# Attention steps inside five product stages: an order written out by hand for TensorE, VectorE and ScalarE

## The chip, the cores and the metric

One core of a Trainium2 chip. The metric is the device time of one launch in microseconds, the median of several runs. The kernel works on five engines that run beside each other: TensorE (matmuls and transposes), VectorE, ScalarE, GpSimd, and SyncE, which only issues transfers. Each takes its own list of instructions in order, and they wait for each other through semaphores.

## What is computed

Attention with a window and sinks, and then a product of two projections, projected again. In the reference (cut):

```
pos = np.arange(S)
keep = (pos[None, :] < n_sink) | ((rel >= 0) & (rel < window))
scores = np.where(keep, scale * q @ k.T, -1e9)
a = np.exp(scores - max); a = a / (a.sum(-1) + 1e-9)
x = (a @ v).transpose(0, 2, 1, 3).reshape(B * S, H * D)
return (x @ w_a) * (x @ w_b) @ w_out
```

B = 4 batches, H = 8 heads, S = 768 positions of D = 64, 4 sinks, a window of 128; so x is 3072 x 512, the hidden width 1536, all float32. To keep float32 accuracy every operand of a product is split in a high and a low part, and three partial products (high high, high low, low high) are summed.

## The kernel before

The 3072 rows are cut into eight chunks, given in tiles of 128 rows (`CHUNKS`; batch, first tile, number of tiles): (0,0,4), (0,4,2), (1,0,3), (2,0,3), (1,3,3), (2,3,3), (3,0,3), (3,3,3). The kernel runs eight **product stages**, one for each chunk, and in each of them the attention of the chunk that follows; only the attention of the first chunk stands ahead, and the last stage has none beside it. The third to seventh stage have 384 rows each.

A product stage (`moe`) goes over the hidden width in twelve blocks j. For each j there are three **groups** of matmuls: a (12 of 384 columns into PSUM tile a, L769), b (the same into tile b), and o (9 of 512 columns into three tiles that hold the output, L778), which belongs to the block before, j - 1. Between them ScalarE copies a to an SBUF tile g (L788), VectorE multiplies it by b (L794), ScalarE casts it to gh (L797), and GpSimd subtracts to get gl (L799; VectorE for the last two blocks). There is one buffer of g, so the copy of the next a waits until gl is done.

The attention of a chunk is a Python generator; `between(s)`, called behind each group, takes steps of it. A step works on **units** (one head and one query tile of 128, 24 in a chunk) in different phases:

- scores: two matmuls s (L485), an s tile in PSUM; the mask (L491) and the maximum with it (L493) on VectorE; exp on ScalarE (L495); the inverse of the sum on VectorE (L497, L498); the scaling on ScalarE (L503) and the scaling of the eight sink columns to sc (L504).
- transposes, two steps later: T (L524) into PSUM tile t. ScalarE copies it within the tile, rounded (L527), and to p (L530); VectorE makes the high part of the product operand pt (L528), the rest (L531) and the low part (L532). These joined units are those of query tile 2 and above; those of tiles 0 and 1 have one or two T (L539), one ScalarE copy (L542) and one VectorE subtraction (L543).
- av, once for a head: matmuls into tile av (L555), and xf from them by a ScalarE copy (L560) and one or two VectorE additions (L561, L563).
- skt and sk, for four heads together: the sink columns transposed (L570; into the PSUM tile that s uses), split (L573 to L575), and multiplied by the sinks' values (L581, added at L583).

All T of a stage use one PSUM bank, s has one bank, av has one. GpSimd rounds and splits the keys, queries and values of a coming head (`prep_kq`, `prep_v`: qh, ks, ql, ks, vv, vv, and vs for every fourth head; L382, L385).

The third, fourth, ... stage differ in the chunk beside them: attention of tiles 0 to 2 (light: 8 units of each tile) in the third and sixth stage, of tiles 3 to 5 (joined: all units) in the fourth, fifth and seventh. The light ones also have loads and checks of the weights (`check_weight`: a reduction on VectorE, a square on ScalarE).

What sets the order of each engine is a scheduler (Tile's): it takes the program's instructions with their dependencies and its own estimates of their durations, and puts an instruction wherever it expects the engine to be free. So matmuls of attention may stand inside a group of products.

Of the kernel before, what the change touches and what calls it, by code (L numbers as in the profile page):

```python
# [31 lines left out]
BIG = 3.0e38  # L32
# [47 lines left out]
def general_path(tc, ident, val, kT, qT, vB, wa, wb, wo, out):  # L80
# [143 lines left out]
class Fast:  # L224
# [14 lines left out]
    def consts(self):  # L239
        nc, cp = self.nc, self.cp  # L240
        self.m0 = cp.tile([P, P], F32, name="m0")
        self.m1 = cp.tile([P, SW], F32, name="m1")
        self.mg = cp.tile([P, SW], F32, name="mg")
        self.rel = rel = self.at.tile([P, SW], F32, tag="p", name="rel")
        self.col = col = self.at.tile([P, SW], F32, tag="p", name="col")
        it = dict(allow_small_or_imprecise_dtypes=True)
        s, b = slice(P, P + NS), slice(P + NS, SW)
        nc.gpsimd.iota(rel[:, b], pattern=[[-1, P]], base=0, channel_multiplier=1, **it)
        nc.gpsimd.iota(rel[:, :P], pattern=[[-1, P]], base=P, channel_multiplier=1, **it)
        nc.gpsimd.iota(rel[:, s], pattern=[[1, NS]], base=0, channel_multiplier=0, **it)  # L250
# [9 lines left out]
        self.pt, self.kr, self.no_gpsimd, self.banks = None, {}, False, ("t",)  # L260
        self.wt, self.raw, self.wf, self.temp, self.unchecked = {}, {}, {}, None, []

    def masks(self, val):

# [119 lines left out]
    def rest(self, o, i, high):  # L384
        (self.nc.vector if self.no_gpsimd else self.nc.gpsimd).tensor_tensor(o, i, high.bitcast(F32), op=ALU.subtract)  # L385
# [70 lines left out]
    def parts_split(self, b, t0, nt, xf, alone, heads, bank):  # L456
# [127 lines left out]

        return do_prep, scores, transposes, av, sinks_t, sinks_av

    def parts_exact(self, b, t0, nt, xf, alone, heads, bank):

        nc = self.nc
        tag = f"{b}_{t0}"  # L590
        s0 = max(t0 - 1, 0)
        nb = t0 + nt - s0
        kw = nb * KB - NS
        late = [i for i in range(nt) if t0 + i >= 2]
        units = [(h, i) for h in heads for i in range(nt)]
        preps, state, sc, vss, pts, skt = {}, {}, {}, {}, {}, {}
# [155 lines left out]
            xs.append((xh, xl))  # L752
        return xs

    def moe(self, row, nt, xf, between, weights_ahead, last, weights_split):
# [24 lines left out]

        prev = None
        for j in range(NJ):
            if last and j == NJ - 2:
                self.ok = self.verdict(self.ps.tile([1, P], F32, tag="s", name="gp"))
            weights_ahead(3 * j)
            pa = half("a", j)
            g = self.mo.tile([P, max(n, 3 * P)], F32, tag="g", name=f"g{tag}_{j}", bufs=1)
            nc.scalar.copy(g[:, :n], pa[:, :n])  # L788
            between(3 * j)
            if last and j == NJ - 1:  # L790
                self.tc.mark_branch_hint_location("general", hint="LikelyTaken", engines=mybir.ALL_ENGINES)
            weights_ahead(3 * j + 1)
            pb = half("b", j)
            nc.vector.tensor_tensor(g[:, :n], pb[:, :n], g[:, :n], op=ALU.mult)  # L794
            gh = self.mo.tile([P, max(n, 3 * P)], F32R, tag="gh", name=f"gh{tag}_{j}")
            gl = self.mo.tile([P, max(n, 3 * P)], F32R, tag="gl", name=f"gl{tag}_{j}")
            nc.scalar.copy(gh[:, :n], g[:, :n])  # L797
            e = nc.gpsimd if weights_split and j < NJ - 2 else nc.vector
            e.tensor_tensor(gl[:, :n], g[:, :n], gh[:, :n].bitcast(F32), op=ALU.subtract)  # L799
            between(3 * j + 1)  # L800
            weights_ahead(3 * j + 2)
            if prev is not None:
                project(*prev)
# [12 lines left out]
    def run(self, scalars, verdict):  # L816
        chunks = CHUNKS
# [35 lines left out]
        b, t0, nt = chunks[0]  # L853
# [11 lines left out]
        for c, (b, t0, nt) in enumerate(chunks):  # L865
            gen = None
            if c + 1 < len(chunks):
                nb, nt0, nnt = chunks[c + 1]
                nxf = self.new_xf(c + 1)

                self.banks = ("t", "o2") if nt == 2 else ("t",)
                if c == 1:
                    self.join_masks()
                gen = (self.attention if c else self.attention_of_two)(nb, nt0, nnt, nxf)
                steps = H * nnt + 6
            taken = [0]
# [22 lines left out]
            self.moe(b * S + t0 * P, nt, xf, between, ahead, c + 1 == len(chunks), c > 1)  # L899
            if gen is not None:  # L900
                for _ in gen:
                    pass
                xf = nxf
# [74 lines left out]
```

## Time and profile before

| | us |
|---|---|
| median of 3 runs (from 793.3 to 794.84) | 794.43 |
| the profiled execution | 793.14 |
| its span, first to last instruction | 791.4 |

The profiled execution is 1.3 us below the median, and 1.7 us of it lie outside its span. The mean granted clock of TensorE is 0.998 of full speed. A group of matmuls in the profile has a modelled end; a start is measured. The third product stage starts at 243.0 us of the span, the fourth at 334.7, the fifth at 429.7, the sixth at 524.8, the seventh at 615.4, the eighth at 710.6.

### The profile page before, as it was taken

The numbers are of one execution on the slowest core, as the hardware profiler recorded it, in microseconds if no ns is written. First come the engines' busy times: TensorE is split into PE (matmuls) and PEld (weight loads), VectorE is DVE, ScalarE is ACT, GpSimd is POOL, SyncE is SP. The second block draws the span as 40 slices with busy tenths as digits, with TensorE's granted clock in tenths as the row PEclk, the third lists the DMA queues.
The fourth block names the chain that finished last, engine by engine and source line by source line (L and its number), as shares of the span: only waits on it lengthen the run. The fifth ranks groups of instructions, "written<-read, shape, count | busy, mean of one in ns | idle before, by whom it ended". The sixth has DMA issues, their size and how long they took to land.

```text
span 791.4 us, 13783 instructions
## 1 busy us (share of the span) xinstructions
PE 774.1 (98%) x4349; PEld 680.7 (86%) x4349; DVE 516.8 (65%) x1759; ACT 477.8 (60%) x1485; POOL 291.6 (37%) x400
## 2 busy tenths in 40 slices
PE   8999999989999999999999999999999999999997
PEld 5768777779799999998889889999999988989996
DVE  6888889977874675467773777636665478643321
ACT  5867577747765776466663766546764566644431
POOL 1110000146652564355660756416445466201110
PEclk9999999999999999999999999999999999999999
DMA  9877400242121332312111111112333112005511
GB/s 321 291 254 278 180 17 1 75 142 58 48 77 41 101 121 91 119 53 62 45 58 51 45 45 48 48 50 86 122 119 101 54 55 64 28 24 185 176 55 43
DMA packets 44573, 75.84 MB, mean 96 GB/s; under 512 B 4592, under 2 KB 24016, under 8 KB 44496
## 3 DMA queue, kind: packets, MB, share of 16 engines
q1 hardware_dynamic: 41440, 69.40, 27.0%
q10 hardware_dynamic: 3024, 5.51, 1.9%
q8 instruction: 36, 0.59, 0.3%
q14 instruction: 41, 0.34, 0.1%
q0 software_dynamic: 32, 0.00, 0.0%
HBM read 68.60 MB, written 6.29 MB: 95 GB/s over the span
## 4 chain that ended last, share of the span: by engine, by line
PE 84%; DVE 10%; ACT 3%; issue 1%; DMA 0%; POOL 0%; DVEq 0%; ACTq 0%; POOLq 0%
PE b L769 23%; PE a L769 23%; PE o L778 22%; PE s L485 4%; PE av L555 4%; PE t L524 2%; PE s L631 2%; PE av L685 1%; PE t L539 1%; DVE wf L343 1%; DVE wf L336 1%; PE t L668 1%; DVE g L794 1%; DVE gl L799 1%; DVE w L353 1%
## 5 line engine op out<-in xcount | busy, mean ns | idle before, releaser
L769 PE MATMUL a<-xh,w 128*128 128x384 f32 (+2 forms) x768 | 215.8, 342 | 0.8 <-ACT w L348 0.8
L769 PE MATMUL b<-xh,w 128*128 128x384 f32 (+2 forms) x768 | 214.6, 341 | 0.0
L778 PE MATMUL o<-w,gh 128*128 128x512 f32 x576 | 186.7, 402 | 0.7 <-ACT gh L797 0.7
L769 PEld LDWEIGHTS a<-xh,w 128*128 128x128 f32 x768 | 138.6, 188 | 6.2 <-ACT w L348 1.1
L769 PEld LDWEIGHTS b<-xh,w 128*128 128x128 f32 x768 | 138.9, 189 | 3.9 <-issue 0.3
L799 POOL TENSOR_TENSOR gl<-g,gh 128x384 fp32r<-128x384 f32 x60 | 61.0, 1016 | 188.4 <-ACT gh L797 186.1
L769 PE MATMUL b<-xl,w 128*128 128x384 f32 (+2 forms) x384 | 130.1, 339 | 0.0
L769 PE MATMUL a<-xl,w 128*128 128x384 f32 (+2 forms) x384 | 129.4, 337 | 0.0
L794 DVE TENSOR_TENSOR g<-b,g 128x384 f32<-128x384 f32 (+2 forms) x96 | 53.2, 554 | 107.2 <-PE b L769 96.7
L778 PEld LDWEIGHTS o<-w,gh 128*128 128x128 f32 x576 | 104.1, 189 | 19.4 <-ACT gh L797 1.3
L778 PE MATMUL o<-w,gl 128*128 128x512 f32 x288 | 114.9, 400 | 0.6 <-DVE gl L799 0.6
L788 ACT COPY g<-a 128x384 f32<-128x384 f32 (+2 forms) x96 | 45.5, 474 | 71.8 <-PE a L769 66.2
L797 ACT CAST gh<-g 128x384 fp32r<-128x384 f32 (+2 forms) x96 | 49.2, 512 | 64.2 <-DVE g L794 62.1
L769 PEld LDWEIGHTS a<-xl,w 128*128 128x128 f32 x384 | 72.4, 189 | 2.7
L495 ACT ACTIVATE p<-p,st 128x264 f32<-128x264 f32 (+1 forms) x152 | 65.5, 431 | 14.2 <-DVE st L493 12.9
L769 PEld LDWEIGHTS b<-xl,w 128*128 128x128 f32 x384 | 72.5, 189 | 1.6
L382 POOL TENSOR_SCALAR ks<-kr 64x400 fp32r<-64x400 f32 (+1 forms) x48 | 28.9, 603 | 107.7 <-DVE pt L543 105.4
L778 PEld LDWEIGHTS o<-w,gl 128*128 128x128 f32 x288 | 54.3, 188 | 13.7 <-DVE gl L799 1.8
L382 POOL TENSOR_SCALAR qh<-qr 128x384 fp32r<-128x384 f32 x48 | 24.9, 518 | 103.9 <-PE s L485 96.5
L385 POOL TENSOR_TENSOR ks<-kr,ks 64x400 fp32r<-64x400 f32 (+1 forms) x48 | 57.9, 1206 | 3.9
L503 ACT ACTIVATE p<-p,st 128x128 f32<-128x128 f32 x96 | 38.7, 403 | 24.4 <-DVE st L498 21.8
L555 PE MATMUL av<-pt,vv 128*128 128x256 f32 (+1 forms) x288 | 50.4, 285 | 0.3
(153 smaller groups left out, 1410.2 us busy)
## 6 DMA issues: line engine op xcount, KB each, us to landing
qr<-in_qT_dram SPq DMA_DIRECT2D x48, 192.0 KB, 2.4
raw<-in_wa_dram SPq DMA_DIRECT2D x12, 512.0 KB, 6.2
raw<-in_wb_dram SPq DMA_DIRECT2D x12, 512.0 KB, 6.7
raw<-in_wo_dram SPq DMA_DIRECT2D x12, 512.0 KB, 6.7
chk_a<-in_wa_dram SPq DMA_DIRECT2D x24, 256.0 KB, 2.7
chk_b<-in_wb_dram SPq DMA_DIRECT2D x24, 256.0 KB, 2.9
chk_o<-in_wo_dram SPq DMA_DIRECT2D x24, 256.0 KB, 2.9
out_dram<-os ACTq DMA_DIRECT2D x21, 256.0 KB, 2.2
```

The lines of the kernel that those rows point to most:

```text
L382: self.nc.gpsimd.tensor_scalar(o, i, 1.0, 1.0, op0=ALU.mult, op1=ALU.mult)
L385: (self.nc.vector if self.no_gpsimd else self.nc.gpsimd).tensor_tensor(o, i, high.bitcast(F32), op=ALU.subtract)
L485: nc.tensor.matmul(ps[:, :w], lhsT=q[:, i * P:(i + 1) * P], rhs=ks[:, c0:c0 + w], start=m == 0, stop=m == 1)
L495: nc.scalar.activation(p[:, :w], p[:, :w], AF.Exp, bias=st[:, 0:1], scale=-1.0, accum_out=st[:, 1:2])
L503: nc.scalar.mul(p[:, NS:KB], p[:, NS:KB], st[:, 3:4])
L555: nc.tensor.matmul(ps[:, cols], lhsT=vv[:, blk, :], rhs=m, start=n == 0, stop=n == len(products) - 1, skip_group_check=True)
L769: nc.tensor.matmul(ps[:, :n], lhsT=w[:, ksl], rhs=x[:, :n], start=kk == 0 and i == 0, stop=kk == NK - 1 and i == 2)
L778: nc.tensor.matmul(outs[i], lhsT=g[:, sl], rhs=w, start=j == 0 and k == 0, stop=j == NJ - 1 and k == 2)
L788: nc.scalar.copy(g[:, :n], pa[:, :n])
L794: nc.vector.tensor_tensor(g[:, :n], pb[:, :n], g[:, :n], op=ALU.mult)
L797: nc.scalar.copy(gh[:, :n], g[:, :n])
L799: e.tensor_tensor(gl[:, :n], g[:, :n], gh[:, :n].bitcast(F32), op=ALU.subtract)
```

## The change

In the third to seventh stage (`given`) TensorE, VectorE and ScalarE are taken out of the scheduler's hands: within `manual_schedule` their instructions stand as the program issues them. GpSimd and SyncE stay with the scheduler. For those stages the attention is a new generator, `steady`. It issues the same instructions as before with the same tiles; its phases are cut in pieces (maximum, exponential, inverse, scale; rounding, split; copy, add), which one loop interleaves. `steady_plan` lists for each step which unit is scored, which is transposed two steps later, and whether av, skt or sk follows: 31 steps behind one of preparation. Step 13 has no scores (it has a T and the first skt). `between` takes one step behind each group, beginning behind the first b group; the last four groups have none. The cast gh and the subtraction gl of a block are no longer issued behind the b group at once, but by `late_act` inside the step that follows it.

```diff
+    def late_act(self):
+        for f in self.later:
+            f()
+        self.later = []
...
+    def steady(self, b, t0, nt, xf):
...
+            def rounding():
+                if t < 2:
+                    A.copy(hs, tp[:, :n, :])
+                    return
+                A.copy(tp[:, 1, :].bitcast(F32R), tp[:, 0, :])
+                A.copy(hj, tp[:, 0, :])
+
+            def split():
+                if t < 2:
+                    V.tensor_tensor(ls, tp[:, :n, :], hs.bitcast(F32), op=ALU.subtract)
+                    return
+                V.tensor_tensor(hs, tp[:, 1:2, :].broadcast_to([P, 2, P]), tri, op=ALU.mult)
+                V.tensor_tensor(tp[:, 0, :], tp[:, 0, :], hj.bitcast(F32), op=ALU.subtract)
+                V.tensor_tensor(ls, tp[:, 0:1, :].broadcast_to([P, 2, P]), tri, op=ALU.mult)
...
+        for score, turn, rest in plan:
+            turned = evicted = ()
+            scored = ()
+            if score is not None:
+                if score[1] == 0:
+                    do_prep(score[0] + 1)
+                scored = scores(*score)
+            if turn is not None:
+                turned = transposes(*turn)
+            if rest is not None:
+                evicted = {"av": av, "skt": sinks_t, "sk": sinks_av}[rest[0]](*rest[1:])
+            if turned:
+                turned[0]()
+            if scored:
+                scored[0]()
+                scored[1]()
+            if turned:
+                turned[1]()
+            self.late_act()
+            if evicted:
+                evicted[0]()
+            if scored:
+                scored[2]()
+                scored[3]()
+            if evicted:
+                evicted[1]()
+            yield
+
+    def steady_plan(self, units, nt):
+
+        gap = 4 * nt + 1
+        at = {}
+        for k, u in enumerate(units):
+            at[u] = k + (k >= gap)
+        rest = {}
+        for h in range(H):
+            rest[at[h, nt - 1] + 3] = ("av", h)
+        for g in range(2):
+            k = at[4 * g + 3, nt - 1] + 2
+            rest[k] = ("skt", g)
...
@@ -794,10 +994,17 @@
-            nc.scalar.copy(gh[:, :n], g[:, :n])
-            e = nc.gpsimd if weights_split and j < NJ - 2 else nc.vector
-            e.tensor_tensor(gl[:, :n], g[:, :n], gh[:, :n].bitcast(F32), op=ALU.subtract)
+
+            def parts(j=j, g=g, gh=gh, gl=gl):
+                nc.scalar.copy(gh[:, :n], g[:, :n])
+                e = nc.gpsimd if weights_split and j < NJ - 2 else nc.vector
+                e.tensor_tensor(gl[:, :n], g[:, :n], gh[:, :n].bitcast(F32), op=ALU.subtract)
+
+            self.later.append(parts)
+            if not given or j == NJ - 1:
+                self.late_act()
             between(3 * j + 1)
+            self.late_act()
...
-                if c:
+                if c > 1:
+                    want = min(steps, -(-steps * (s + (s < 2)) // (3 * NJ - 3)))
+                elif c:
...
+            given = 1 < c < len(chunks) - 1
+            with ExitStack() as ctx:
+                if given:
+                    E = mybir.EngineType
+                    ctx.enter_context(self.tc.manual_schedule(engines={E.PE, E.DVE, E.Activation}))
```

**TensorE, fourth stage, block 3: the b group and what follows.** Names are those of the tiles: a, b and o are the product tiles, s, t and av those of attention; t1_3 with p1_3_2_0 is T of head 2, tile 0 of the chunk; x2 means twice in a row. Before, from the end of the s pair behind group a:

```order
L555 MATMUL av1_3_1_4550<-pt_1439,vv1_1_3_4261 128x256
L769 MATMUL b1536_3_4567<-xh1536_0_4179,w4_878 128x384
L769 MATMUL b1536_3_4567<-xl1536_0_4180,w4_878 128x384
L524 MATMUL t1_3_0_0_4318<-ident_58,p1_3_1_2_4422 128x128
L555 MATMUL av1_3_1_4550<-pt_1439,vv1_1_3_4261 128x256
L769 MATMUL b1536_3_4567<-xh1536_0_4179,w4_878 128x384
L769 MATMUL b1536_3_4567<-xh1536_1_4183,w4_878 128x384
L769 MATMUL b1536_3_4567<-xl1536_1_4184,w4_878 128x384
L769 MATMUL b1536_3_4567<-xh1536_1_4183,w4_878 128x384
L769 MATMUL b1536_3_4567<-xh1536_2_4187,w4_878 128x384
L555 MATMUL av1_3_1_4550<-pt_1439,vv1_1_3_4261 128x256
L769 MATMUL b1536_3_4567<-xl1536_2_4188,w4_878 128x384
```

After, from the last matmul of b:

```order
L969 MATMUL b1536_3_4543<-xh1536_3_4196,w4_878 128x384
L617 MATMUL s1_3_2_2_4559<-ks1_2_3_4361,qh1_2_3_4362 128x264
L617 MATMUL s1_3_2_2_4559<-ks1_2_3_4361,ql1_2_3_4363 128x264
L661 MATMUL t1_3_4331<-ident_58,p1_3_2_0_4495 128x128
L697 MATMUL av1_3_1_4565<-pt_1439,vv1_1_3_4264 128x256 x5
L697 MATMUL av1_3_1_4565<-pt_1439,vv1_1_3_4264 128x128 x2
L978 MATMUL o1536_0_4200<-w5_929,gh1536_2_4438 128x512 x2
L978 MATMUL o1536_0_4200<-w5_929,gl1536_2_4439 128x512
L978 MATMUL o1536_1_4201<-w5_929,gh1536_2_4438 128x512 x2
L978 MATMUL o1536_1_4201<-w5_929,gl1536_2_4439 128x512
L978 MATMUL o1536_2_4202<-w5_929,gh1536_2_4438 128x512 x2
L978 MATMUL o1536_2_4202<-w5_929,gl1536_2_4439 128x512
```

Before, T and three av products stand between the matmuls of b, and the s pair of this step ahead of them; after, b is whole, and s, T and the seven av products follow it in one piece, and then o.

**ScalarE, the same block: the cast gh and its neighbours** (t and p are the two copies of T). Before:

```order
L797 CAST gh1536_3_4581<-g1536_3_4536 128x384
L560 COPY xf4_0_4175<-av1_3_1_4550 64x384
L527 CAST t1_3_0_0_4318<-t1_3_0_0_4318 128x128
L530 CAST p1_3_2_0_4481<-t1_3_0_0_4318 128x128
L527 CAST t1_3_0_0_4318<-t1_3_0_0_4318 128x128
L495 ACTIVATE p1_3_3_0_4618,st1_3_3_0_4619<-p1_3_3_0_4618,st1_3_3_0_4619 128x136
L530 CAST p1_3_2_1_4508<-t1_3_0_0_4318 128x128
L503 ACTIVATE p1_3_3_0_4618<-p1_3_3_0_4618,st1_3_3_0_4619 128x128
L504 ACTIVATE sc1_3_0_0_4274<-p1_3_3_0_4618,st1_3_3_0_4619 128x8
L788 COPY g1536_4_4646<-a1536_4_4633 128x384
```

After:

```order
L675 CAST p1_3_2_0_4495<-t1_3_4331 128x128
L632 ACTIVATE p1_3_2_2_4562,st1_3_2_2_4563<-p1_3_2_2_4562,st1_3_2_2_4563 128x136
L999 CAST gh1536_3_4557<-g1536_3_4523 128x384
L704 COPY xf4_0_4178<-av1_3_1_4565 64x384
L642 ACTIVATE p1_3_2_2_4562<-p1_3_2_2_4562,st1_3_2_2_4563 128x128
L645 ACTIVATE sc1_3_0_2_4346<-p1_3_2_2_4562,st1_3_2_2_4563 128x8
L674 CAST t1_3_4331<-t1_3_4331 128x128
L675 CAST p1_3_2_1_4528<-t1_3_4331 128x128
L632 ACTIVATE p1_3_3_0_4623,st1_3_3_0_4624<-p1_3_3_0_4623,st1_3_3_0_4624 128x136
L642 ACTIVATE p1_3_3_0_4623<-p1_3_3_0_4623,st1_3_3_0_4624 128x128
L645 ACTIVATE sc1_3_0_0_4280<-p1_3_3_0_4623,st1_3_3_0_4624 128x8
L988 COPY g1536_4_4651<-a1536_4_4638 128x384
```

The cast gh and the xf copy stood ahead of the copy of T (L527); now both copies of T and exp (L632) come first, then gh and the xf copy, then the scalings. The g copy stands ahead of the T copies in a's step, now as before.

**GpSimd, the same block: gl and its neighbours** (vv1_3_3 is the value operand of head 3). Before:

```order
L382 TENSOR_SCALAR ks1_4_3_4598<-kr1_4_3_4594 64x536
L385 TENSOR_TENSOR ql1_4_3_4600<-qr1_4_3_4596,qh1_4_3_4599 128x384
L385 TENSOR_TENSOR ks1_4_3_4598<-kr1_4_3_4594,ks1_4_3_4598 64x536
L382 TENSOR_SCALAR vv1_3_3_4475<-vr1_2_3_4354 128x4x64
L799 TENSOR_TENSOR gl1536_3_4582<-g1536_3_4536,gh1536_3_4581 128x384
L385 TENSOR_TENSOR vv1_3_3_4475<-vr1_2_3_4354,vv1_3_3_4475 128x4x64
```

After:

```order
L390 TENSOR_TENSOR ql1_4_3_4605<-qr1_4_3_4601,qh1_4_3_4604 128x384
L390 TENSOR_TENSOR ks1_4_3_4603<-kr1_4_3_4599,ks1_4_3_4603 64x536
L387 TENSOR_SCALAR vv1_3_3_4489<-vr1_2_3_4368 128x4x64
L390 TENSOR_TENSOR vv1_3_3_4489<-vr1_2_3_4368,vv1_3_3_4489 128x4x64
L1001 TENSOR_TENSOR gl1536_3_4558<-g1536_3_4523,gh1536_3_4557 128x384
L387 TENSOR_SCALAR qh1_5_3_4730<-qr1_5_3_4727 128x384
```

The subtraction gl stood between the two operations of vv, and now stands behind both.

## Rows read from the trace of the kernel before

**Rows 1.** The page, busy time of each engine: us, share of the span, instructions.

```profile
PE 774.1 (98%) x4349; PEld 680.7 (86%) x4349; DVE 516.8 (65%) x1759; ACT 477.8 (60%) x1485; POOL 291.6 (37%) x400
```

**Rows 2.** The table by stage: start and end (us), length, then busy us (and instructions) of TensorE, its weight loads, VectorE, ScalarE and GpSimd, granted TensorE clock, DMA share, GB/s. The first five rows are the third to the seventh product stage, the sixth is the eighth.

```profile
243.00:334.70 91.70, 91.67 (x527) 85.17 (x525) 53.39 (x202) 58.40 (x192) 45.38 (x62) 1.00 0.31 99
334.70:429.70 95.00, 94.14 (x535) 84.66 (x535) 62.91 (x232) 56.42 (x188) 48.85 (x62) 1.00 0.18 51
429.70:524.80 95.10, 94.25 (x537) 84.77 (x536) 62.94 (x232) 56.49 (x188) 47.65 (x62) 1.00 0.17 49
524.80:615.40 90.60, 90.60 (x523) 84.52 (x522) 53.48 (x202) 57.95 (x192) 45.40 (x62) 1.00 0.33 102
615.40:710.60 95.20, 94.34 (x536) 84.76 (x535) 63.50 (x234) 56.53 (x188) 38.53 (x48) 1.00 0.14 42
710.60:785.00 74.40, 74.40 (x396) 69.57 (x395) 20.22 (x58) 28.26 (x99) 10.20 (x10) 1.00 0.35 117
```

**Rows 3.** The chain of waits, followed back inside two short stretches of the fourth stage (334.4 to 345 us and 352 to 356 us): start, us, what and how often in a row.

```profile
334.68 2.08 PE a L769 x12
...
338.85 0.24 PE s L485 x2
...
342.50 0.11 PE t L524
...
352.75 2.10 PE o L778 x9
```

**Rows 4.** The timeline of TensorE in the fourth stage: start, us, what; in brackets idle time before it and what ended it.

```profile
357.48 0.28 PE L485 MATMUL s<-ks,ql 128*128 128x264 f32 x1
...
360.94 0.30 PE L524 MATMUL t<-ident,p 128*128 128x128 f32 x1
...
363.90 0.34 PE L769 MATMUL a<-xl,w 128*128 128x384 f32 x1
364.68 0.30 PE L524 MATMUL t<-ident,p 128*128 128x128 f32 x1 [0.45 <-DVE pt L532]
...
368.92 0.93 PE L555 MATMUL av<-pt,vv 128*128 128x256 f32 x7
369.68 0.30 PE L524 MATMUL t<-ident,p 128*128 128x128 f32 x1
```

**Rows 5.** The timeline of ScalarE, the same stretch, columns as in rows 4.

```profile
357.81 0.46 ACT L788 COPY g<-a 128x384 f32<-128x384 f32 x1
...
358.61 0.41 ACT L495 ACTIVATE p<-p,st 128x136 f32<-128x136 f32 x1
358.92 0.19 ACT L495 ACTIVATION_READ_ACCUMULATOR p<-p,st 128x1 f32 x1
359.19 0.27 ACT L530 CAST p<-t 128x128 fp32r<-128x128 f32 x1
359.59 0.40 ACT L503 ACTIVATE p<-p,st 128x128 f32<-128x128 f32 x1
359.90 0.28 ACT L504 ACTIVATE sc<-p,st 128x8 f32<-128x8 f32 x1
361.17 0.52 ACT L797 CAST gh<-g 128x384 fp32r<-128x384 f32 x1 [0.99 <-DVE g L794]
361.71 0.47 ACT L560 COPY xf<-av 64x384 f32<-64x384 f32 x1
362.08 0.26 ACT L527 CAST t<-t 128x128 fp32r<-128x128 f32 x1
...
365.02 0.25 ACT L527 CAST t<-t 128x128 fp32r<-128x128 f32 x1 [1.50 <-PE t L524]
```

**Rows 6.** The timeline of VectorE, the same stretch, columns as in rows 4.

```profile
358.73 0.42 DVE L528 TENSOR_TENSOR pt<-t,tri 128x256 fp32r<-128x256 f32 x1 [0.22 <-ACT t L527]
359.14 0.15 DVE L497 TENSOR_SCALAR st<-st 128x1 f32<-128x1 f32 x1
359.33 0.16 DVE L498 RECIPROCAL st<-st 128x1 f32<-128x1 f32 x1
359.49 0.30 DVE L531 TENSOR_TENSOR t<-t,p 128x128 f32<-128x128 f32 x1
359.82 0.42 DVE L532 TENSOR_TENSOR pt<-t,tri 128x256 fp32r<-128x256 f32 x1
360.58 0.56 DVE L794 TENSOR_TENSOR g<-b,g 128x384 f32<-128x384 f32 x1 [0.34 <-PE b L769]
...
364.11 0.42 DVE L532 TENSOR_TENSOR pt<-t,tri 128x256 fp32r<-128x256 f32 x1
```

**Rows 7.** The timeline of GpSimd, the same stretch, columns as in rows 4.

```profile
357.80 0.51 POOL L382 TENSOR_SCALAR qh<-qr 128x384 fp32r<-128x384 f32 x1 [0.94 <-POOL vs L385]
...
359.95 1.33 POOL L385 TENSOR_TENSOR ks<-kr,ks 64x536 fp32r<-64x536 f32 x1
361.37 0.40 POOL L382 TENSOR_SCALAR vv<-vr 128x256 fp32r<-128x256 f32 x1
361.77 1.01 POOL L799 TENSOR_TENSOR gl<-g,gh 128x384 fp32r<-128x384 f32 x1
362.73 0.74 POOL L385 TENSOR_TENSOR vv<-vr,vv 128x256 fp32r<-128x256 f32 x1
```

More of the change, by code (lines that the diff above doesn't have):

```diff
@@ L259, in consts @@
         V.memset(self.m1[:, s], -NEG)
-        self.pt, self.kr, self.no_gpsimd, self.banks = None, {}, False, ("t",)
+        self.pt, self.kr, self.no_gpsimd, self.banks, self.later = None, {}, False, ("t",), []
         self.wt, self.raw, self.wf, self.temp, self.unchecked = {}, {}, {}, None, []
+    def late_act(self):
+        for f in self.later:
+            f()
+        self.later = []
     def masks(self, val):
@@ L585, in parts_split, with do_prep, scores, maximum @@
         return do_prep, scores, transposes, av, sinks_t, sinks_av
+    def steady(self, b, t0, nt, xf):
+        nc = self.nc
+        V, A, T = nc.vector, nc.scalar, nc.tensor
+        tag = f"{b}_{t0}"
+        s0 = max(t0 - 1, 0)
+        late = [i for i in range(nt) if t0 + i >= 2]
+        cols = len(late) * P
+        xs = slice(late[0] * P, nt * P)
+        units = [(h, i) for h in range(H) for i in range(nt)]
+        preps, state, sc, vss, skt, bank = {}, {}, {}, {}, {}, []
+        def do_prep(h):
+            if h < H:
+                preps[h] = *self.prep_kq(b, h, t0, nt), self.prep_v(b, h, t0, nt)
+                if h % 4 == 0:
+                    vss[h // 4] = self.vs
+        def scores(h, i):
+            ks, qh, ql, _ = preps[h]
+            t = t0 + i
+            u = f"{tag}_{h}_{i}"
+            c0 = (max(t - 1, 0) - s0) * KB
+            w = SW if t else P
+            ps = self.ps.tile([P, SW], F32, tag="s", name=f"s{u}")
+            for m, q in enumerate((qh, ql)):
+                T.matmul(ps[:, :w], lhsT=q[:, i * P:(i + 1) * P], rhs=ks[:, c0:c0 + w], start=m == 0, stop=m == 1)
+            p = self.at.tile([P, SW], F32, tag="p", name=f"p{u}")
+            st = self.at.tile([P, 4], F32, tag="st", name=f"st{u}")
+            state[h, i] = p
+            def maximum():
+                x, y, n = ps, (self.m0, self.m1, self.mg)[min(t, 2)], w
+                if t > 1:
+                    V.copy_predicated(ps[:, KB:], self.up, ps[:, :P])
+                    x, y, n = ps[:, P:], y[:, P:], KB
+                V.tensor_tensor_reduce(out=p[:, :n], in0=x[:, :n], in1=y, scale=-0.125, scalar=BIG,
+                                       op0=ALU.add, op1=ALU.min, accum_out=st[:, 0:1])
+            def exponential():
+                n = KB if t > 1 else w
+                A.activation(p[:, :n], p[:, :n], AF.Exp, bias=st[:, 0:1], scale=-1.0, accum_out=st[:, 1:2])
+            def inverse():
+                V.tensor_scalar(st[:, 2:3], st[:, 1:2], 1e-9, None, op0=ALU.add)
+                V.reciprocal(st[:, 3:4], st[:, 2:3])
+            def scale():
+                if t < 2:
+                    A.mul(p[:, :w], p[:, :w], st[:, 3:4])
+                    return
+                A.mul(p[:, NS:KB], p[:, NS:KB], st[:, 3:4])
+                if h % 4 == 0:
+                    sc[h // 4, i] = self.at.tile([P, 4, NS], F32, tag=f"sc{i}", name=f"sc{u}", bufs=2)
+                A.mul(sc[h // 4, i][:, h % 4, :], p[:, :NS], st[:, 3:4])
+            return maximum, exponential, inverse, scale
+        def transposes(h, i):
+            p = state.pop((h, i))
+            t = t0 + i
+            n = units.index((h, i))
+            if not bank:
+                bank.append(self.ps.tile([P, 4, P], F32, tag="t", name=f"t{tag}"))
+            tp = bank[0][:, 2 * (n % 2):2 * (n % 2) + 2, :]
+            c1, c2, order = UNITS[nt][i]
+            parts = {"A": p[:, :P], "B": p[:, P + NS:]}
+            if t == 0:
+                order, parts["B"] = "B", p[:, :P]
+            if t > 1:
+                T.transpose(tp[:, 0, :], p[:, NS:KB], self.ident)
+            else:
+                for k, o in enumerate(order):
+                    T.transpose(tp[:, k, :], parts[o], self.ident)
+            n = len(order)
+            hs, ls = (self.pt_split()[:, part, c1:c1 + (n - 1) * (c2 - c1) + 1:c2 - c1, :] for part in range(2))
+            hj = p[:, NS:KB].bitcast(F32R)
+            tri = self.tri if order == "AB" else self.tri[:, ::-1]
+            def rounding():
[5 more added lines that the diff above has]
+            def split():
+                if t < 2:
+                    V.tensor_tensor(ls, tp[:, :n, :], hs.bitcast(F32), op=ALU.subtract)
+                    return
+                V.tensor_tensor(hs, tp[:, 1:2, :].broadcast_to([P, 2, P]), tri, op=ALU.mult)
+                V.tensor_tensor(tp[:, 0, :], tp[:, 0, :], hj.bitcast(F32), op=ALU.subtract)
+                V.tensor_tensor(ls, tp[:, 0:1, :].broadcast_to([P, 2, P]), tri, op=ALU.mult)
+            return rounding, split
+        def av(h):
+            vv = preps[h][3]
+            ps = self.ps.tile([P, 4 * P], F32, tag="av", name=f"av{tag}_{h}")
+            pt = self.pt_split()
+            products = []
+            for k, sl, ns, c in GROUPS[nt]:
+                if t0 + k >= 0:
+                    moving = [pt[:, part, sl:sl + ns, :] for part in range(2)] if ns else [pt[:, :, sl, :]]
+                    products += [(t0 + k - s0, m, slice(c * P, (c + (ns or 2)) * P)) for m in moving]
+            for n, (blk, m, c) in enumerate(products):
+                T.matmul(ps[:, c], lhsT=vv[:, blk, :], rhs=m,
+                         start=n == 0, stop=n == len(products) - 1, skip_group_check=True)
+            x = xf[h // 2]
+            n = nt * P
+            mn, mi = self.halves(h)
+            def copy():
+                A.copy(x[mn, :n], ps[mi, :n])
+            def add():
+                V.tensor_tensor(x[mn, :n], ps[mn, :n], x[mn, :n], op=ALU.add)
+                V.tensor_tensor(x[mn, 2 * P:], ps[mn, 3 * P:], x[mn, 2 * P:], op=ALU.add)
+            return copy, add
+        def sinks_t(g):
+            tp = self.ps.tile([4 * NS, 3 * P], F32, tag="s", name=f"skt{tag}_{g}")
+            for k, i in enumerate(late):
+                T.transpose(tp[:, k * P:(k + 1) * P], sc[g, i].rearrange("p a b -> p (a b)"), self.ident)
+            s = self.at.tile([P, 3 * P], F32R, tag="sct", name=f"sct{tag}_{g}", bufs=1)
+            q = 4 * NS
+            skt[g] = s
+            def copy():
+                A.copy(s[:q, :cols], tp[:, :cols])
+            def rest():
+                V.tensor_tensor(s[q:D, :cols], tp[:, :cols], s[:q, :cols].bitcast(F32), op=ALU.subtract)
+                A.copy(s[D:, :cols], s[:D, :cols].bitcast(F32))
+            return copy, rest
+        def sinks_av(g, pr):
+            ps = self.ps.tile([P, 4 * P], F32, tag="av", name=f"sk{tag}_{g}_{pr}")
+            T.matmul(ps[:, :cols], lhsT=vss[g][:, pr, :], rhs=skt[g][:, :cols], start=True, stop=True)
+            x = xf[2 * g + pr][:, xs]
+            return (lambda: None), (lambda: V.tensor_tensor(x, ps[:, :cols], x, op=ALU.add))
+        plan = self.steady_plan(units, nt)
+        do_prep(0)
+        yield
[25 more added lines that the diff above has]
+                evicted[1]()
+            yield
@@ new lines, in steady_plan @@
+    def steady_plan(self, units, nt):
[9 more added lines that the diff above has]
+            rest[k] = ("skt", g)
+            for pr in range(2):
+                while k in rest or k <= at[4 * g + 3, nt - 1] + 4:
+                    k += 1
+                rest[k] = ("sk", g, pr)
+        score = {k: u for u, k in at.items()}
+        turn = {k + 2: u for u, k in at.items()}
+        n = max(*rest, *turn) + 1
+        return [(score.get(k), turn.get(k), rest.get(k)) for k in range(n)]
@@ L753, in split_x, with moe @@
         return xs
-    def moe(self, row, nt, xf, between, weights_ahead, last, weights_split):
+    def moe(self, row, nt, xf, between, weights_ahead, last, weights_split, given):
         nc = self.nc
@@ L873, in run @@
                     self.join_masks()
-                gen = (self.attention if c else self.attention_of_two)(nb, nt0, nnt, nxf)
+                gen = (self.attention_of_two, self.attention, self.steady)[min(c, 2)](nb, nt0, nnt, nxf)
                 steps = H * nnt + 6
+                if c > 1:
+                    steps = 1 + len(self.steady_plan([(h, i) for h in range(H) for i in range(nnt)], nnt))
             taken = [0]
@@ L897, in ahead @@
                     self.check_weight(None, 0)
[L899 to L903, printed above, removed]
+            given = 1 < c < len(chunks) - 1
[3 more added lines that the diff above has]
+                    ctx.enter_context(self.tc.manual_schedule(engines={E.PE, E.DVE, E.Activation}))
+                self.moe(b * S + t0 * P, nt, xf, between, ahead, c + 1 == len(chunks), c > 1, given)
+                if gen is not None:
+                    for _ in gen:
+                        pass
+                    xf = nxf
         return val, self.ok
```

1 line of the change is left out of this document (added).

## The prediction

> **What bounds the kernel now.** I read the busy line first: TensorE is busy 98% of the span, VectorE 65%, ScalarE 60%, GpSimd 37% [rows 1]. Then the table by stage [rows 2]: its first five rows are the stages that the change touches, the sixth is the last product stage, which runs the same products with no attention beside it. The granted clock is 1.00 in all six (the 2.4 GHz level), so no term of the clock enters. By busy time, TensorE idles for only 0.0 + 0.9 + 0.9 + 0.0 + 0.9 = 2.6 us in the five stages. But ends of matmuls are modelled, so what is lost must be read from starts.
>
> What a stage must cost: twelve 384-column matmuls take 2.08 us, nine 512-column ones 2.10 [rows 3]. A row j has groups a, b and o: 2 x 2.08 + 2.10 = 6.26 us, twelve rows 75.1 (the last stage, without attention, has 74.4 in its window). Of attention, a stage adds 24 steps with a pair of s products (0.24) and a transpose T (0.11) [rows 3], and 8 times seven av products (368.92 to 369.68, 0.76 [rows 4]). A joined stage (attention on query tiles 3 to 5, those of 95 us) has 24 x 0.35 + 8 x 0.76 + six skt transposes 0.7 + four sk products 0.7 = 15.9. So 95.0 - 75.1 - 15.9 = 4.0 us of the stage from 334.70 are late starts, and 4.1 and 4.2 of the other two. A light stage (tiles 0 to 2) has 16 wide and 8 narrow s pairs (0.24 and, half as wide, some 0.12), 34 transposes (0.11), 8 x 0.6 of av and 0.2 of sk: 13.5. That leaves 2.0 of the 90.6, and 2.4 of the 91.7 (less 0.7 for three o products of the stage ahead that fall into its window). Together 16.7 us, 2% of the span, is all that any order can win.
>
> The Trainium skill (Perfetto Trace Analysis, Identifying the Most-Contended Engine) says that busy time of matmuls is no good measure of how near TensorE is to its limit, since they are pipelined. The trace agrees: 2.6 us by busy time against 16.7 by starts; by busy time alone the most that the change could give would be 2.6.
>
> **What makes starts late.** All T of a stage share one PSUM bank, so a T waits until VectorE's third split (L532) of the T before it has ended. At 364.68 T starts 0.45 late for that [rows 4]: L532 ran from 364.11 to 364.53 [rows 6]. ScalarE is behind it: T had started at 360.94, and its first copy (L527) usually follows after 0.34 (364.68 to 365.02), but came at 362.08, because gh (361.17 to 361.69) and the xf copy (361.71 to 362.18) stood ahead of it in ScalarE's order [rows 5]. T also stands anywhere within a group of products, so T to T is now short, now long.
>
> **The change part by part.** No instruction is added or removed. GpSimd and SP keep a scheduler. Three things move.
>
> First, T stands behind every product group, directly after the s pair: TensorE meets it every 2.08 + 0.35 = 2.43 us, with av once in three steps; a row of three steps takes 6.26 + 1.05 + 0.76 = 8.07.
>
> Second, both copies now stand ahead of VectorE's splits, and gh and the xf copy behind exp. What T to T needs: copy 0.25, copy 0.27 [rows 5], splits 0.42, 0.30, 0.42 [rows 6], with four handovers of 0.03 is 1.78; T to the copy 0.34 and last split to T 0.15 (364.53 to 364.68) make 2.27, under the 2.43. But ScalarE must come round too: after the third split the two inverse steps (0.15 and 0.16, the first overlapping by 0.08, 0.26 in all), then 0.10 to the scaling (359.49 to 359.59), 0.31 to the sc scaling, 0.28 for that, less 0.09 overlap with the next copy: 2.64 a step. In a's step the g copy (0.46, of which 0.37 counts) stands ahead of the copies: 3.01. Three steps: 8.29. Exp, gh and xf (0.41 + 0.19 for reading its sum, 0.52, 0.47, overlapping to some 1.35 [rows 5]) lie inside the 1.6 that splits and inverse take, so they cost nothing; cover 0.25. In four of eight rows this loop decides, at 8.29 against 8.07: 0.22 x 4 = 0.9.
>
> Third, the late cast: gl on GpSimd now stands behind both vv operations, where it stood between them. The g copy of the next row must wait for gl (one g buffer). In the first half of a joined stage GpSimd starts qh when the s of b's step has ended (357.80 behind the s of 357.48 [rows 4, 7]), 0.2 after T there; then 3.57 to vv (361.37), 0.40, 0.82 for the second vv (0.74 and 0.08 of turn), 1.01 for gl: 6.0; g copy 0.08 later, 0.37, 1.78 and 0.15 to the next T of b's step: 8.38. Four rows at 0.3 over 8.07: 1.2. In the second half of a stage a step without a score has shifted the units by one step against the groups, qh starts behind o's step, and gl has that time in hand; I count nothing there.
>
> Sinks: skt uses the bank of s. Its subtract (0.55) stands behind the third split in the fixed order and ends 0.34 + 1.78 + 0.55 = 2.7 after T; the next s is reached after 0.33 + 2.08 = 2.4, so 0.3, or up to 0.7 where copies are already late: 0.7 for a stage. Each second sk waits for the first one's add, 2.9 against 2.6: 0.4. The 0.47 and 0.55 of these come from the xf copy and g product, as wide [rows 5, 6]. Small lags of a T directly behind narrow products add 0.3.
>
> Sum of a joined stage: 0.9 + 1.2 + 0.7 + 0.4 + 0.3 = 3.5, against 4.0, 4.1 and 4.2: gains 0.5 + 0.6 + 0.7 = 1.8. A light stage has less work in the loop (16 of 24 units have one copy and one split instead of two and three; VectorE 53.5 us against 62.9 [rows 2]), so that I let no step bind; left are T behind T behind a narrow s (some 0.07 x 8), sinks 0.4, and 0.2: 1.2 against 2.4 and 2.0, gains 2.0. The weight checks of these stages stand in the order behind a's step; their loads are issued a group or more ahead, and I take nothing for them; 18 late ones of 0.1 would cost 1.8, which the range holds.
>
> Total 3.8 us. The profiled execution takes 793.1, so 789.3; the median of the runs is 1.3 above it: **790.6**.
>
> **Rivals.** A, slower: the fixed ScalarE and VectorE order binds every joined row. Its price: each 0.1 us on a row costs 0.1 x 8 x 3 = 2.4, so the gain of 3.8 is used up at 0.16 a row. VectorE does the g product (0.56 [rows 6]) ahead of the mask and maximum in b's step, exp comes later by that, and the cover of 0.25 can be gone: then 0.25 more a row is +6.0 - 3.8 = +2.2, 796.6. For it: the pile of 361.17 to 362.18 shows what one cast ahead costs. Against: gh is behind the copies now.
>
> The Trainium skill (PSUM — Partial Sum Buffer, Engine vs sequencer instructions) says that ScalarE, VectorE and GpSimd take their queues strictly in order; a hand order then lets whoever waits at the head hold all behind it. The 362.08 above agrees; that mechanism is A.
>
> B, much faster: the row's 8.29 and 8.38 have slack that I counted twice, TensorE alone sets 8.07. Joined stages keep sinks and lags, 1.4: gains 2.6 + 2.7 + 2.8, with the light 2.0 about 10: 784.4. For it: T to T of 2.27 is all that TensorE itself needs; against: ScalarE's 2.64 is longer than 2.43.
>
> C, no change: what is won at T comes back at gl on GpSimd and at the sinks, and the light stages win half: 793 to 795. The same time comes out if gl's later place costs all of 0.4 a row.
>
> **How the numbers follow.** Forecast (787 to 792.8) 0.48, B 0.13, C 0.21, A 0.18. A measurement of this kernel can tell 0.2% (1.6 us) from no change. Faster 0.61, same 0.21, slower 0.18. The range goes down to B's 784.5 and up to 797.0, just past A; some 0.15 is outside.
>
> **What would show it.** In the joined stages T every 2.43 to 3.0 us with ScalarE and VectorE as what it waits for; stage lengths 94.4 to 94.6 (now 95.0 to 95.2), light ones 89.8 and 90.5; T's wait for VectorE larger in total than now but spread evenly; g copies waiting for GpSimd's gl in the first half of joined stages only; the last stage unchanged at 74.4. Joined stages above 95.5 mean A; below 93 mean B; light stages that don't shorten would mean that I mis-sized their losses.

## The result and the profile after

The changed kernel takes 800.31 us (median of 4 runs, 799.79 to 800.83) against 794.63 for the kernel before (4 runs): a ratio of 1.0074, 95% interval 1.0057 to 1.0091. It is slower by 5.7 us; 790.6 was forecast and the range ended at 797.0.

The page after: the busy line, and the chain of work that ended last, by engine. The first line answers to [rows 1]; in the kernel before, the chain read PE 84%, DVE 10%, ACT 3%.

```profile
PE 774.2 (97%) x4349; PEld 686.3 (86%) x4349; DVE 525.0 (66%) x1759; ACT 475.4 (59%) x1485; POOL 292.2 (37%) x400
...
PE 59%; DVE 23%; ACT 10%; issue 3%; POOL 2%; DMA 2%; ACTq 0%; DVEq 0%; POOLq 0%
```

Busy times have hardly moved, but a third of the chain now runs through VectorE and ScalarE: TensorE is waited for less and waits more. The table by stage, columns as in [rows 2]:

```profile
244.20:336.30 92.10, 91.48 (x527) 85.13 (x526) 54.39 (x203) 58.36 (x192) 45.56 (x62) 1.00 0.32 98
336.30:433.00 96.70, 94.13 (x536) 86.36 (x535) 64.86 (x232) 55.41 (x188) 49.05 (x62) 1.00 0.17 50
433.00:529.70 96.70, 94.13 (x536) 86.36 (x535) 64.87 (x232) 55.36 (x188) 47.88 (x62) 1.00 0.17 48
529.70:621.10 91.40, 90.67 (x523) 84.47 (x522) 54.37 (x202) 58.06 (x192) 45.52 (x62) 1.00 0.33 102
621.10:718.00 96.90, 94.30 (x536) 86.38 (x536) 65.52 (x234) 55.47 (x188) 38.77 (x48) 1.00 0.13 41
718.00:792.40 74.40, 74.40 (x395) 69.57 (x394) 20.25 (x58) 28.51 (x99) 10.21 (x10) 1.00 0.35 117
```

Against [rows 2] the five changed stages are 0.4, 1.7, 1.6, 0.8 and 1.7 us longer, 6.2 together; the last is unchanged at 74.4, and so is the granted clock. (The profiled execution, 800.83, is the slowest of the four; 1.2 us of its distance to the one before lies ahead of the third stage, where the order is the same.) So all five stages lost, the light ones too.

Where a joined stage loses is seen in one row of it. TensorE in the fourth stage after, columns as in [rows 4]:

```profile
358.98 0.27 PE L661 MATMUL t<-ident,p 128*128 128x128 f32 x1
...
361.30 0.29 PE L617 MATMUL s<-ks,ql 128*128 128x264 f32 x1
361.82 0.30 PE L661 MATMUL t<-ident,p 128*128 128x128 f32 x1 [0.23 <-DVE st L635]
361.88 1.02 PE L697 MATMUL av<-pt,vv 128*128 128x256 f32 x7
362.73 0.68 PE L978 MATMUL o<-w,gh 128*128 128x512 f32 x2
...
365.12 0.27 PE L661 MATMUL t<-ident,p 128*128 128x128 f32 x1
```

T behind a's group (358.98) is on time; T behind b's (361.82) follows s 0.52 after its start instead of 0.12: 0.4 late. T behind o's is on time again. The profile names L635 as the releaser, but T needs the third split, which ended just ahead of it, at 361.67. VectorE, the same stretch:

```profile
358.22 0.42 DVE L683 TENSOR_TENSOR pt<-t,tri 128x256 fp32r<-128x256 f32 x1
358.56 0.15 DVE L635 TENSOR_SCALAR st<-st 128x1 f32<-128x1 f32 x1
358.74 0.16 DVE L636 RECIPROCAL st<-st 128x1 f32<-128x1 f32 x1
...
360.46 0.42 DVE L681 TENSOR_TENSOR pt<-t,tri 128x256 fp32r<-128x256 f32 x1 [0.64 <-ACT p L675]
...
361.25 0.42 DVE L683 TENSOR_TENSOR pt<-t,tri 128x256 fp32r<-128x256 f32 x1
```

VectorE was idle for 0.64 until ScalarE had made the copies. ScalarE:

```profile
356.84 0.25 ACT L674 CAST t<-t 128x128 fp32r<-128x128 f32 x1
357.13 0.27 ACT L675 CAST p<-t 128x128 fp32r<-128x128 f32 x1
...
359.00 0.41 ACT L642 ACTIVATE p<-p,st 128x128 f32<-128x128 f32 x1 [1.07 <-DVE st L636]
359.31 0.29 ACT L645 ACTIVATE sc<-p,st 128x8 f32<-128x8 f32 x1
359.50 0.46 ACT L988 COPY g<-a 128x384 f32<-128x384 f32 x1
359.86 0.27 ACT L674 CAST t<-t 128x128 fp32r<-128x128 f32 x1
360.15 0.27 ACT L675 CAST p<-t 128x128 fp32r<-128x128 f32 x1
```

ScalarE stood idle 1.07 until VectorE's inverse (358.74 to 358.90), which the written order puts behind the third split; then come the scalings, the g copy, and only then the copy of a T that had started at 358.98 and could have been copied at 359.32. Copy to copy takes 359.86 - 356.84 = 3.02, TensorE's step 2.43. That this wait is the rule shows in ScalarE's waits in this stage: who waited for whom, us in total, times, longest.

```profile
ACT p L642 <- DVE st L636: 18.9, 23, 1.2
...
ACT g L988 <- POOL gl L1001: 0.5, 1, 0.5
```

The scalings waited for the inverse at nearly every step, 18.9 us; the g copy waited for GpSimd once. In the same stage of the kernel before, the wait of the scalings was this:

```profile
ACT p L503 <- DVE st L498: 4.0, 9, 0.7
```

There the scheduler had put the inverse between the first and the second split (359.14 and 359.33 in [rows 6]).

### The profile page after: what moved, and what is told of

It reads as the page before. It is cut to its first block, busy times and chain, and to the rows that moved or that the text cites. A ratio compares the mean times of both kernels' runs of the same rounds, so it can differ in the third digit from the quotient of the medians.

```text
span 799.1 us, 13885 instructions
## 1 busy us (share of the span) xinstructions
PE 774.2 (97%) x4349; PEld 686.3 (86%) x4349; DVE 525.0 (66%) x1759; ACT 475.4 (59%) x1485; POOL 292.2 (37%) x400
## 4 chain that ended last, share of the span: by engine, by line
PE 59%; DVE 23%; ACT 10%; issue 3%; POOL 2%; DMA 2%; ACTq 0%; DVEq 0%; POOLq 0%
PE a L969 16%; PE o L978 16%; PE b L969 14%; DVE pt L681 3%; DVE pt L683 3%; DVE t L682 2%; PE av L697 2%; PE s L831 2%; PE s L617 2%; ACT p L675 2%; ACT g L988 1%; PE av L885 1%; ACT p L642 1%; DVE st L636 1%; ACT sc L645 1%
## 5 line engine op out<-in xcount | busy, mean ns | idle before, releaser
L642 ACT ACTIVATE p<-p,st 128x128 f32<-128x128 f32 x88 | 35.6, 405 | 58.2 <-DVE st L636 57.7
L632 ACT ACTIVATE p<-p,st 128x136 f32<-128x136 f32 (+2 forms) x120 | 51.2, 426 | 26.0 <-DVE st L627 24.5
L681 DVE TENSOR_TENSOR pt<-t,tri 128x256 fp32r<-128x256 f32 x88 | 37.3, 424 | 33.0 <-ACT p L675 30.3
```

Source lines behind the costliest of these rows:

```text
L632: A.activation(p[:, :n], p[:, :n], AF.Exp, bias=st[:, 0:1], scale=-1.0, accum_out=st[:, 1:2])
L642: A.mul(p[:, NS:KB], p[:, NS:KB], st[:, 3:4])
L681: V.tensor_tensor(hs, tp[:, 1:2, :].broadcast_to([P, 2, P]), tri, op=ALU.mult)
```

## The experiments

The theory after the result: ScalarE and VectorE go round once a step (copies, splits, inverse, scalings, next copies), and with the g copy that round is longer than TensorE's step. The rivals: GpSimd's late gl; the plan itself (one step a group); the late cast. Each experiment's median is set against the kernel before in the same runs (793.3 to 793.4); the row of the change has its own runs, against 794.63 as above. So a difference in microseconds between the change and an experiment can be off by a microsecond; the stage lengths beside it don't hang on that. The two columns at the right are the fourth (joined) and sixth (light) stage in the profile, from the first a product of a stage to that of the next.

| kernel | median us | ratio to before, 95% | fourth | sixth |
|---|---|---|---|---|
| before | 793.3 | | 95.05 | 90.67 |
| the change | 800.31 | 1.0074 (1.0057 to 1.0091) | 96.70 | 91.45 |
| e1 g copy later | 791.58 | 0.9976 (0.9967 to 0.9986) | 94.45 | 90.65 |
| e2 scalings later | 795.34 | 1.0034 (1.0020 to 1.0049) | 94.62 | 92.03 |
| e3 both | 789.47 | 0.9954 (0.9938 to 0.9971) | 92.90 | 91.78 |
| e4 scheduler | 788.89 | 0.9942 (0.9925 to 0.9958) | 93.83 | 90.48 |
| e5 inverse between | 795.00 | 1.0020 (1.0008 to 1.0031) | 95.03 | 91.37 |
| e6 inverse and g copy | 790.13 | 0.9952 (0.9934 to 0.9970) | 93.70 | 91.04 |
| e7 joined by hand | 785.94 | 0.9901 (0.9884 to 0.9919) | 92.90 | 90.07 |
| e8 cast at once | 812.93 | 1.0241 (1.0222 to 1.0259) | 99.88 | 93.35 |
| e9 scheduler, cast at once | 788.35 | 0.9934 (0.9916 to 0.9953) | 93.80 | 90.47 |
| e10 before, cast later | 792.89 | 0.9991 (0.9982 to 1.0001) | 95.02 | 90.55 |
| e11 narrow av earlier | 785.70 | 0.9900 (0.9881 to 0.9918) | 92.87 | 90.10 |

**e1, the g copy behind exp.**

```diff
-            nc.scalar.copy(g[:, :n], pa[:, :n])
+            self.later.append(lambda g=g, pa=pa: nc.scalar.copy(g[:, :n], pa[:, :n]))
...
             between(3 * j)
+            self.late_act()
```

> In a's step ScalarE makes the g copy behind exp instead of ahead of the two T copies. Theory (step by step): the T behind group b is 0.42 late because the chain copy to copy takes 3.02 in a's step and the slack of the step with av can't be saved for it; without the g copy the chain is 2.65, T is late by under 0.1, each joined stage loses 1.5 to 2.5 us less: 793 to 796. Rival (GpSimd): T behind b waits for gl through the g copy; then nothing changes, 800.

791.58, 8.7 us less than the change (8.3 by the stages), and below the 793 to 796 that were expected: one ScalarE copy at another place is more than the whole loss. The GpSimd rival falls. All five stages gain: a joined one 2.25 to 2.3, as expected, and the light ones, for which the forecast had nothing, 0.7 to 0.8.

**e2, the scalings behind the next step's copies; e3, both.**

```diff
             if turned:
                 turned[0]()
+            while waiting:
+                waiting.pop()()
...
-                scored[3]()
+                waiting.append(scored[3])
```

> The two scalings of a unit stand behind the T copies of the following step, so ScalarE no longer waits for VectorE's inverse within a step; the g copy stays ahead of the copies. Theory (step by step): the chain copy to copy is broken, T is late at no step but those of the sinks, joined stages lose 2.5 to 3 us less: 790 to 793. Rival (GpSimd): 800, as before the edit.

> Both edits together. Theory: as with the scalings alone, at most 0.5 us a stage better, 789 to 793, since either edit alone takes the lateness behind b away. If the two gains add up in full (786 to 789), there are two chains and not one.

e2 missed on the slow side: joined stages gain 2.1 (2.5 to 3 expected) and light ones lose 0.6 to 0.8. In e3 joined stages gain 3.8, where the single gains are 2.25 and 2.1. So they nearly add; that either edit alone would take the lateness away was wrong. Without the g copy the round (2.65 from copy to copy in e1) is still over 2.43, and with the scalings away the g copy is still ahead of the copies. With both, ScalarE waits for TensorE instead of the reverse. Its waits in the fourth stage of e3:

```profile
ACT t L674 <- PE t L661: 20.7, 24, 1.5
```

At all 24 steps the copy waited for T; in the change without the edits it did at 2. In the light stages the squares of the weight checks show up ahead of the copies. ScalarE in the sixth stage of the change itself, where T had started at 578.48:

```profile
578.39 0.44 ACT L367 ACTIVATE chk_o<-chk_o 128x256 f32<-128x256 f32 x1
578.73 0.19 ACT L367 ACTIVATION_READ_ACCUMULATOR chk_o<-chk_o 128x1 f32 x1
578.82 0.43 ACT L367 ACTIVATE chk_o<-chk_o 128x256 f32<-128x256 f32 x1
579.14 0.20 ACT L367 ACTIVATION_READ_ACCUMULATOR chk_o<-chk_o 128x1 f32 x1
579.24 0.27 ACT L674 CAST t<-t 128x128 fp32r<-128x128 f32 x1
```

The copy comes 0.42 late; the next T starts 0.16 late and the av behind it some 0.3 more. This is not the hand order's alone: in e4, under the scheduler, copies of T stand behind squares too, up to 1.27 after their T in the sixth stage (1.47 in the change). No run took the checks out of the way alone, so what they cost in all stays open, as does why e2 makes light stages longer.

**e4, the new plan and the late cast under the scheduler.** Only the entry into `manual_schedule` is taken out.

```diff
-                if given:
-                    E = mybir.EngineType
-                    ctx.enter_context(self.tc.manual_schedule(engines={E.PE, E.DVE, E.Activation}))
```

> The new generator, its plan and the late cast, but TensorE, VectorE and ScalarE left to the scheduler in these stages. If the written order costs the time: 792 to 796, like the kernel before. If the plan or the late cast costs it (one step a group, gl late): 799 to 802.

788.89, better than either forecast: the plan wins 4.4 us, and writing the order by hand costs some 11 (11.4 by the medians, 10.9 by the five stages). ScalarE in e4, a's step:

```profile
355.38 0.25 ACT L674 CAST t<-t 128x128 fp32r<-128x128 f32 x1
355.66 0.27 ACT L675 CAST p<-t 128x128 fp32r<-128x128 f32 x1
...
356.87 0.40 ACT L642 ACTIVATE p<-p,st 128x128 f32<-128x128 f32 x1 [0.55 <-DVE st L636]
357.18 0.28 ACT L645 ACTIVATE sc<-p,st 128x8 f32<-128x8 f32 x1
357.37 0.46 ACT L988 COPY g<-a 128x384 f32<-128x384 f32 x1
357.73 0.27 ACT L674 CAST t<-t 128x128 fp32r<-128x128 f32 x1
```

The same instructions on ScalarE in the same order, the g copy ahead too, but copy to copy takes 2.35 and not 3.02: the scaling starts 1.49 behind the first copy and not 2.16, because here VectorE's inverse stands behind the first and second split. VectorE, the same step:

```profile
355.95 0.42 DVE L681 TENSOR_TENSOR pt<-t,tri 128x256 fp32r<-128x256 f32 x1 [0.53 <-ACT p L675]
356.36 0.15 DVE L635 TENSOR_SCALAR st<-st 128x1 f32<-128x1 f32 x1
356.43 0.29 DVE L682 TENSOR_TENSOR t<-t,p 128x128 f32<-128x128 f32 x1
356.62 0.15 DVE L636 RECIPROCAL st<-st 128x1 f32<-128x1 f32 x1
356.75 0.42 DVE L683 TENSOR_TENSOR pt<-t,tri 128x256 fp32r<-128x256 f32 x1
```

**e5, that one placement by hand; e6, with the g copy later.**

```diff
-            if turned:
-                turned[1]()
+            between = list(scored[2]) if scored else []
+            for _ in turned[1]() if turned else ():
+                if between:
+                    between.pop(0)()
```

(`split` yields behind the first and the second split, `inverse` is a pair.)

> One placement of the written order changed: VectorE's two inverse steps stand behind the first and the second split of T instead of behind the third, where the scheduler puts them with the same plan (its joined stages took 93.8 us against 96.7). Theory (the inverse at the end of the step holds back the scalings and, in ScalarE's order, the next copies): copy to copy in a's step falls from 3.0 to some 2.4 to 2.6 us, joined stages to 93.8 to 94.5, light ones to 90.3 to 91: 789 to 793. Rival (the scheduler wins elsewhere): no change, 799 to 801.

> The inverse between the splits, and the g copy behind exp. Theory (one chain, ScalarE's way round): the g copy adds little once the inverse is early, 0 to 1 us a stage: 786 to 791. If the g copy is a cost of its own, it adds its full 2.2 us a joined stage: below 786.

795.0: the inverse alone gives back 1.6 us a joined stage, a little over half of the 2.9 that lie between the change and e4, and nothing in the light ones, so the forecast was missed on the slow side. With the g copy later too, 790.1, inside the range of the one-chain theory, though joined stages gain 1.1 to 1.3 by it (0 to 1 expected, 2.2 by the rival): a part of the g copy's cost is its own. The fourth stage takes 93.7, as under the scheduler (93.8), and what is left between e6 and e4 lies mostly in the light stages.

**e7, joined stages by hand with both edits of e3, light stages under the scheduler.** The entry into `manual_schedule` reads `if given and nt0:`; the edits of e3 hold for the joined stages alone.

> Joined stages with both earlier edits (g copy and scalings later, 92.9 us each by hand), light stages with the new plan but left to the scheduler (90.0 and 90.5). Stages add up, since nothing is carried over a stage's end: 789.5 - 1.6 - 1.3 = 786.6 (785.5 to 787.5). If what a stage wins is given back in the next, 788 to 790.

785.94, as expected: the stages add up. It is 1.0% faster than the kernel before and 1.8% faster than the change. Its fourth stage:

```profile
334.60:427.50 92.90, 92.80 (x535) 86.31 (x535) 65.36 (x232) 53.32 (x188) 49.07 (x62) 1.00 0.17 52
```

Against 96.70 of the change with the same instructions, the 3.8 us are TensorE's waits.

**e8, the cast not late.**

```diff
-            if not given or j == NJ - 1:
-                self.late_act()
+            self.late_act()
```

> The written order, but the cast gh and the subtraction gl directly behind VectorE's g product, ahead of the T copies of b's step, as the kernel before issued them. If the late cast is right for this order (step by step theory): in the second half of a joined stage the step behind b has no av to cover 0.43 of cast, so 0.3 to 0.4 for each of four rows: joined stages 1 to 1.6 longer, 802 to 806. If the late gl was a cost (my rival C, GpSimd): shorter, 796 to 799.

812.93, the right sign at more than twice the size: joined stages are 3.2 to 3.8 longer, and the light ones, for which nothing was expected, 1.6 and 1.9. ScalarE in e8, b's step, where T started at 362.97:

```profile
363.18 0.40 ACT L642 ACTIVATE p<-p,st 128x128 f32<-128x128 f32 x1 [1.21 <-DVE st L636]
363.49 0.29 ACT L645 ACTIVATE sc<-p,st 128x8 f32<-128x8 f32 x1
363.68 0.50 ACT L999 CAST gh<-g 128x384 fp32r<-128x384 f32 x1
364.08 0.26 ACT L674 CAST t<-t 128x128 fp32r<-128x128 f32 x1
```

The cast stands in the same round as the g copy does in a's step, and the lateness reaches a's T as well (0.15 to 0.4 in four rows). So with the written order the late cast is right, and the rival that gl comes too late on GpSimd is wrong in its sign.

**e9 and e10, the late cast apart from the hand order.** e9 is e4 with the cast at once; e10 is the kernel before with `between(3 * j + 1)` moved ahead of gh and gl in the third to seventh stage.

> The new plan under the scheduler, with gh and gl issued directly behind the g product. Splits what the plan under the scheduler wins over the kernel before (788.9 against 793.3) between the plan's steps and the late cast. If the late cast carries it: joined stages back near 95, 792 to 794. If the steps carry it, or the scheduler finds the later place by itself: 788 to 790.

> The kernel before with one thing changed, gh and gl issued behind the attention step that follows group b instead of ahead of it, the scheduler as before. If the late cast by itself is worth something (the T at 364.68 us of the kernel before was late behind gh and the xf copy): joined stages 0.3 to 1 us shorter each, 790 to 792.5. If it needs the new plan: 793 to 794.

788.35 and 792.89: under the scheduler the late cast changes nothing that can be told, with either plan. In e9 the scheduler puts gh behind both T copies by itself. So what e4 wins comes from the plan's steps and the order in which they are issued. Whether it is T's place behind the group that wins is not shown: of the 24 T of a joined stage 18 stand inside a group in the kernel before, 7 in e4 and e9, and none by hand; in the light stages, which e4 shortens by 0.8 and 0.2, none does in the kernel before.

**e11, the two narrow av products not last**, on top of e7.

```diff
-            for k, sl, ns, c in GROUPS[nt]:
+            g0, g1, g2, g3 = GROUPS[nt]
+            for k, sl, ns, c in (g0, g3, g1, g2):
```

> On top of the joined stages by hand and light stages by the scheduler (785.9): the two 128-column av products of a head stand in third and fourth place instead of last. If the 0.10 that the two matmuls behind av start late is weight load which a 0.06 us product is too short to hide: 0.1 for each of eight heads, 0.8 a joined stage, 783.5. If any av costs this much where product types change: no change, 785.5 to 786.5.

785.70: no change. By starts the two lags of 0.05 have moved along, from the o products to the av products that now follow the narrow ones; the sum is the same. My reading that a wider product would hide them was wrong.

## Why the prediction was wrong

The sum of a joined stage is the step that failed, in the T and sink terms above all: it let the long step with av make up for rounds that last longer than TensorE's short steps. It forecast 3.5 us of late starts against 4.0 before. By starts (each matmul against the start of the one before plus its issue cost) the fourth stage has 6.2 after and 4.5 before; the issue costs sum to 90.5 here, where the prediction had 91.0. By its terms:

- **T, 0.9 + 1.2 forecast, 2.8 measured.** The size is not far off, by luck, since the mechanism is half wrong. I averaged the round over three steps (8.29 against 8.07), but steps are coupled one by one: the slack of the step with av (3.2 long) cannot be saved, and a's 3.02 against 2.43 is paid in b's T, 0.4 a row in the first half (0.16, 0.56, 0.40 and 0.56). Of T's lateness 1.1 is left in e1 and 0.2 in e3. The 1.2 for GpSimd's gl is nothing: the g copy waited for it once, 0.5.
- **Sinks, 0.7 + 0.4 forecast, 2.5 measured.** I counted them from a T that is copied on time. The copies were 0.7 late (T 376.12, copy 377.18), and the subtract ended at 379.58, so s waited 0.8 in one place (by starts it is 0.97 late, in e1 0.60, in e3 0.22, so most of it is the late copies):

```profile
376.12 0.30 PE L661 MATMUL t<-ident,p 128*128 128x128 f32 x1
...
378.49 0.34 PE L969 MATMUL b<-xh,w 128*128 128x384 f32 x1
379.63 0.39 PE L617 MATMUL s<-ks,qh 128*128 128x264 f32 x1 [0.81 <-DVE sct L724]
```

- **Lags behind narrow products, 0.3 forecast, 0.8 measured**, the two starts of 0.05 behind each of eight av.
- **Light stages, a gain of 2.0 forecast, a loss of 1.2 measured.** "I let no step bind" was wrong: the g copy binds there too (e1 takes 0.7 to 0.8 off each), and the weight checks, for which I took nothing, hold copies up, at a cost that stays open.

Rival A had the mechanism, in-order queues on ScalarE and VectorE that bind every joined row, and the sign; it had the place wrong: not exp late behind the g product in b's step, but the scalings behind the inverse, and the g copy, in a's. Its 796.6 was 3.7 short. e1, e2 and e5 show the place: in the fourth stage the whole loss against the kernel before (95.05) goes when the g copy (e1, 94.45), the scalings (e2, 94.62) or the inverse (e5, 95.03) is moved. The Trainium skill (PSUM — Partial Sum Buffer, Engine vs sequencer instructions) says that ScalarE takes its queue strictly in order; the 1.07 at 359.00 agrees: the scalings waited at the head, and the T copy that could have been made at 359.32 came behind them and the g copy, at 359.86. Rival B came nearest to what is there to win, though not for this order: e7 wins 7.5 against the kernel before in its runs, where B had 10. Of rival C, GpSimd is out, and the sinks were right (2.5 instead of 1.1). What the new plan gives under the scheduler, 4.4 us (e4), is near the 3.8 forecast for the whole, by coincidence, since the forecast's terms were those of the written order; the price of that order, some 11, is what I missed, since I priced each step's chain from durations and let the lateness of one step end with it.

## What to carry to other kernels

Where two engines hand work back and forth once a step, write out the round (copy, splits, inverse, scaling, next copy) and compare it with each single step of the bound engine, not with the mean of several: here the slack of a long step was not carried to the next. What stands ahead of the handover on a queue lengthens the round, so work that nobody waits for soon (a copy for a product one step away, a scaling needed two steps later) goes behind it. A good plan and a good order inside its steps are two changes: measure the plan under the scheduler first, as e4 did, and write out by hand only stages where that is shown to win.

## What the runs showed of the hardware

A 128-column product costs TensorE more than its own issue of 0.06 us: the two matmuls behind a pair of them start 0.05 late each, wherever the pair stands (e11), so each costs some 0.11, as a T does. And a joined stage of e7 takes 92.9 us where issue costs sum to 90.5: TensorE is within 3% of what its own matmuls need while ScalarE is busy for 53.32 us of it and VectorE for 65.36.
